# Gated linear attention with a seven-product matmul: sums of weights moved from GpSimd to VectorE, one weight load moved ahead of the operand fetches, small stores spread

## The chip, the cores and the metric

The kernel runs on one core of one Trainium2 chip. The core has TensorE (matmuls, results in PSUM banks), VectorE (DVE in the profile), ScalarE (ACT), GpSimd (POOL) and SyncE (SP), which here issues all DMAs, in one queue. The metric is the device time of one execution in microseconds.

## The reference

x is 2048 x 1024 float32. It is normalized by rows, and two branches read the result:

```python
xn = _layernorm(x, axis=-1)
s = _A_ref(xn, A_wqkv, A_w_phi, A_wo)      # attention branch
g = _silu(_B_ref(xn, B_w1, B_w3, B_w2))    # gated feed-forward branch
return x + s * g
...
# _A_ref: 32 heads of 32; phi_k likewise from k
pq = jnp.einsum("bhsd,hdf->bhsf", q, w_phi)
phi_q = jnp.concatenate([_softmax(pq, axis=-1), _softmax(-pq, axis=-1)], axis=-1)
kv = jnp.einsum("bhsf,bhsd->bhfd", phi_k, v)
z  = jnp.einsum("bhsf->bhf", phi_k)
o = num / den                              # phi_q with kv, and with z
...
# _B_ref: w1, w3 are 1024 x 3584, w2 is 3584 x 1024
h = _silu(gate) * up
out = jnp.einsum("bsf,fd->bsd", h, w2)
```

## The kernel before

Each float32 operand is split in two fp32r parts, hi and lo (`split`, L89 to L92: ScalarE copies hi, VectorE subtracts it from the source for lo), and a product is made in three passes: hi by hi, hi by lo, lo by hi. The large products use a scheme of seven products for a 2 x 2 block product instead of eight (`ORDER`): the left operands are A11, A12, S2, S1, S3, S4, A22, the right ones B11, B21, T2, T1, T3, B22, T4, where S and T are sums and differences of blocks. `b_sums` makes T3 and T2 out of raw blocks, and two more subtractions in `b_operands`, in place, make T1 and T4. All four stood on GpSimd.

Gate and up together are one 2 x 2 product. The 2048 rows come in two halves (tb), and in each half 28 blocks of 128 hidden columns (f) are worked through, seven products each, twelve matmuls of 128 x 512 a product. The 392 products are numbered as steps 0 to 391. At the start of the second half the products of its first two blocks alternate (`PAIRED`): steps 196, 197, 199 belong to block 0, step 198 is the first product (A11 with B11) of block 1, step 204 its fourth (S1 with T1). Partial results stay in PSUM banks a, b, c: bank b takes four of the seven products in turn, so between two of them a copy (h0, u0) on ScalarE or a sum on VectorE (u1, L631 before, L640 after) has to read it, else the next product waits.

From step 7 on every engine works in the order in which the program is written, step by step (`in_order`, `manual_schedule`): in a step first come the loads, then the matmuls, then splits of right operands four steps ahead (two ahead for block 1 of the second half), then side work, then the copies out of PSUM. The sums of a block stand two steps ahead of its first split (one step for blocks 1 and 2 of the second half). Raw weights (w1, w3) are loaded by `b_load` into the two buffers of pool rw, a block in advance.

Side work is laid between: normalizing and splitting the second half's x (`side_x`), folding the feature map into key and query weights (`side_fold`), sums and splits of key and value weights (`side_kv`) in the first half; the down weights (`side_w2`, 14 units of 11 steps; the first starts at step 197, raw blocks in tiles named room) and the output weights (`side_split`) in the second. `room(step, cost)` puts a piece on the first step whose VectorE work, by a table `base` and what was laid there already, leaves enough under a limit. At the turn between the halves `fetch` loads the second half's seven left operands, 2 MB each, into tiles that the first half's operands leave one by one.

Then come keys and values with 16 small matrices kv (`heads`, `kv_out`), the down product, with its own scheduler-given order, in rows r of eight pairs by seven groups (`product`; `a_first` loads h a row ahead), the queries and the output.

Of the kernel before, what the change touches and what calls it, by code (L numbers as in the profile page):

```python
# [17 lines left out]
P = 128  # L18
# [10 lines left out]
def tile_kernel(ctx: ExitStack, tc: tile.TileContext, x, wkT, wqT, wv, wphi, wo, w1, w3, w2, out):  # L29
# [94 lines left out]
    def b_sums(b11, b12, b22, t2):  # L124

        nc.gpsimd.tensor_sub(b12, b22, b12)
        nc.gpsimd.tensor_add(t2, b12, b11)
# [132 lines left out]
    def b_operands(rw, bo):  # L260
        b11, b21, b12, b22 = rw
        t2 = work.tile([P, 512], F, name="t2", tag="w")
        b_sums(b11, b12, b22, t2)
# [32 lines left out]
    b_gen = b_operands(rws.pop(0), bo)  # L296
# [8 lines left out]
    def first_folds(n):  # L305
        nonlocal at_fold
        for _ in range(n):
            wT, k, c, d = folds[at_fold]
            wr = early_w.pop(0) if early_w else load_w(wT, k, c, work.tile([P, 4, P], F, name="wr", tag="w"))
# [78 lines left out]
    HALF = 7 * NF  # L388
# [8 lines left out]
    for tb in range(2):  # L397
        for f in range(NF):
            own = [at_event[tb, f, j] for j in range(7)]
            steps = [k - LEAD for k in own]  # L400
            if (tb, f) == (1, 1):
                steps = [k - 2 for k in own]
            elif (tb, f) == (1, 2):
                steps = [own[0] + k for k in (-2, -2, -1, 0, 1, 2, 2)]
            if (tb, f) != (0, 0):
                for k in steps:
                    prep_at.setdefault(k, []).append((tb, f))
                sums_at.setdefault(steps[0] - (1 if tb and f in (1, 2) else 2), []).append((tb, f))
            late = divmod(NF * tb + f + 2, NF)
            if late[0] < 2:  # L410
                load_at.setdefault(max(steps[6] + 1, 0) if (tb, f) != (0, 0) else 0, []).append(late)

    base = {k: 0.7 * len(v) for k, v in prep_at.items()}
    for k, (tb, f, j) in enumerate(events):
        base[k + 1] = base.get(k + 1, 0) + (0, 0.7, 0, 0, 0.7, 1.4, 1.4 if f % 2 else 0.7)[j]
# [9 lines left out]
    def store_quad(step, d, src, name):  # L425

        step = room(step, 0.7)

        def f():
            t = qp.tile(list(src().shape[:1]) + [2] + list(src().shape[1:]), R, name=name, tag="q")  # L430
            split(t[:, 0], t[:, 1], src())
            at(step + 2, lambda: nc.sync.dma_start(d, t.bitcast(F)))
# [3 lines left out]
    def side_x(i, s0):  # L436
# [9 lines left out]
        for j in range(2):  # L446
            at_ = room(at_ + 1, 1.6)
# [14 lines left out]
        at_ = max(at_ + 1, s1 + 7)  # L462
        for m in range(3):
            at(at_ + m, lambda m=m: a_sums(a, nc.gpsimd, m))
        at_ += 1
# [3 lines left out]
    def side_kv(c, k, s0):  # L469
# [7 lines left out]
        at(s0 + 4, sums)  # L477
        at_ = s0 + 5
        for n in BNAMES:
            src = {"B11": 0, "B21": 1, "T2": 4, "T1": 0, "T3": 2, "B22": 3, "T4": 1}[n]  # L480
            at_ = store_quad(at_ + 1, wkv_d[c][n][:, :, k], lambda src=src: (r + t2)[src], "wkvo")
            if n == "B11":
                at(at_, lambda: nc.gpsimd.tensor_sub(r[0], r[3], t2[0]))
            elif n == "B21":
                at(at_, lambda: nc.gpsimd.tensor_sub(r[1], r[1], t2[0]))
# [22 lines left out]
    def side_w2(kb, kk, s0):  # L508
# [14 lines left out]
        at(s0 + 3, sums)  # L523
        at_ = s0 + 4
        for n in BNAMES:
            src = {"B11": 0, "B21": 1, "T2": 4, "T1": 0, "T3": 2, "B22": 3, "T4": 1}[n]
            at_ = store_quad(at_ + 1, w2_d[kb][n][:, kk], lambda src=src: r[src], "w2o")
            if n == "B11":
                at(at_, lambda: nc.gpsimd.tensor_sub(r[0], r[3], r[4]))
            elif n == "B21":  # L530
                at(at_, lambda: nc.gpsimd.tensor_sub(r[1], r[1], r[4]))
# [39 lines left out]
    for step, (tb, f, j) in enumerate(events):  # L571
# [108 lines left out]
    pkv = None  # L680

    def heads(i, xo, wb, steps, pend):
# [3 lines left out]
        for b, an, bn in ORDER:  # L686
# [19 lines left out]
            elif an == "S1":  # L706
                if pend:
                    kv(*pend)
                    if first:
                        kv_out(0, pkv)  # L710
# [13 lines left out]
            next(steps)  # L724
        return pkv, False, last, e1, v1

    def kv_out(c, pkv):
        kva = work.tile([P, 8, DH], F, name="kva", tag="w")
# [5 lines left out]
        for s in range(2):  # L734
            for j in range(4):
                sl = slice(32 * j, 32 * j + 32)
                nc.sync.dma_start(kv_d[j % 2, s, :, G * c + j // 2:G * c + G:2], kva[sl, 4 * s:4 * s + 4])
                nc.sync.dma_start(z_d[0, c, :, j, s].rearrange("g f -> f g"), zs[sl, 4 * s:4 * s + 4])

# [194 lines left out]
    for r, new in enumerate(steps):  # L934
# [156 lines left out]
```

## Time and profile before

| | us |
|---|---|
| median of 3 runs | 2465.31 (2465.04 to 2466.66) |
| the profiled execution, device time | 2466.53 |
| its span in the profile | 2464.8 |
| TensorE busy | 2406.8 (98%) |
| VectorE busy | 1748.6 (71%) |
| ScalarE busy | 887.4 (36%) |
| GpSimd busy | 681.8 (28%) |
| DMA | 521 MB moved, 211 GB/s mean |

The granted clock of TensorE was 0.996 of full speed in the mean. A line of a profile names the source line, the engine, the operation and the tiles as written<-read. In the view of groups the last column is the idle time of the engine before these instructions and who ended it; in the timeline the columns are start, duration, engine, line, operation, tiles, shape, count, and in brackets the idle time before and its releaser. A busy TensorE is not one at its peak, since matmuls are pipelined.

### The profile page before, as it was taken

To read this page: it belongs to the slowest core of one execution; us is meant where nothing else is said; L and a number is where in the kernel's file an instruction comes from. 1 tells how busy PE (TensorE), PEld (TensorE's weight loads), DVE (VectorE), ACT (ScalarE), POOL (GpSimd) and SP (SyncE) were. 2 spreads that over 40 slices of the span, in tenths; PEclk is the share of its full clock that TensorE was granted. 3 is DMA by queue.
4 is the path that set the end of the run, shared out by engine and by line. 5 is a ranking of instruction groups with operands and counts; after the bars stand their busy time and mean duration, and the time that the engine had idled before them with its cause. 6 is when DMAs were issued, how large, how long until landed. Compare 5 with 4: busy or idle time off the path is not lost.

```text
span 2464.8 us, 35933 instructions
## 1 busy us (share of the span) xinstructions
PE 2406.8 (98%) x13648; PEld 1971.2 (80%) x13648; DVE 1748.6 (71%) x2573; ACT 887.4 (36%) x1555; POOL 681.8 (28%) x481
## 2 busy tenths in 40 slices
PE   5999999999999999999999999999999999999999
PEld 5788788888788888888788788788888887777877
DVE  8578876664688888764566565687878887777775
ACT  6455544443354454432111113422222244222221
POOL 2334554432455555431000000011111112232222
PEclk9999999999999999999999999999999999999999
DMA  8556999775988887755967763623444376223222
GB/s 296 170 198 228 328 320 303 260 230 175 303 296 293 288 296 278 247 179 199 354 211 297 271 204 123 235 95 138 179 171 180 109 280 232 93 73 92 76 86 69
DMA packets 300812, 521.02 MB, mean 211 GB/s; under 512 B 24544, under 2 KB 172000, under 8 KB 298848
## 3 DMA queue, kind: packets, MB, share of 16 engines
q1 hardware_dynamic: 300640, 518.74, 61.1%
q8 instruction: 107, 1.75, 0.3%
q14 instruction: 65, 0.53, 0.1%
HBM read 331.22 MB, written 187.44 MB: 210 GB/s over the span
## 4 chain that ended last, share of the span: by engine, by line
PE 84%; DVE 6%; DMA 4%; SPq 2%; issue 2%; ACT 1%; POOL 1%; ACTq 0%; DVEq 0%; POOLq 0%
PE bankb L598 19%; PE pm L100 14%; PE bankb L915 12%; PE bankc L598 9%; PE bankb L692 7%; PE bankc L915 6%; PE banka L598 5%; PE bankc L692 3%; PE banka L915 3%; PE banka L692 2%; DVE bo L92 1%; PE po L1019 1%; PE pt L1013 1%; PE pkv L677 1%; DMA xoA<-xo_d0A 1%
## 5 line engine op out<-in xcount | busy, mean ns | idle before, releaser
L92 DVE TENSOR_TENSOR bo<-rw,bo 128x512 fp32r<-128x512 f32 x336 | 289.0, 863 | 214.9 <-ACT bo L91 212.6
L91 ACT CAST bo<-rw 128x512 fp32r<-128x512 f32 x336 | 206.9, 618 | 47.7 <-DMA rw<-in_w 8.8
L915 PE MATMUL bankb<-bo,as 128*128 128x512 f32 x816 | 201.6, 390 | 3.8 <-DVE acc L927 3.8
L925 POOL TENSOR_TENSOR acc<-acc,u 128x512 f32<-128x512 f32 x48 | 63.3, 1319 | 481.0 <-ACT u L924 472.6
L100 PE MATMUL pm<-wq,xh 128*128 128x512 f32 x768 | 185.7, 394 | 0.0
L270 POOL TENSOR_TENSOR rw<-rw,t 128x512 f32<-128x512 f32 x56 | 82.2, 1467 | 370.0 <-DVE bo L92 369.8
L915 PEld LDWEIGHTS bankb<-bo,as 128*128 128x128 f32 x816 | 153.3, 188 | 36.0 <-DVE acc L927 4.2
L598 PE MATMUL bankb<-op1A,bo 128*128 128x512 f32 x672 | 159.7, 393 | 8.9 <-ACT bo L91 4.7
L598 PE MATMUL bankb<-op0A,bo 128*128 128x512 f32 x672 | 160.9, 392 | 7.6 <-ACT bo L91 4.5
L598 PE MATMUL bankb<-op0S,bo 128*128 128x512 f32 x672 | 162.8, 391 | 4.8 <-ACT u L623 4.0
L100 PEld LDWEIGHTS pm<-wq,xh 128*128 128x128 f32 x768 | 141.9, 188 | 31.5 <-issue 3.0
L598 PE MATMUL bankc<-op0S,bo 128*128 128x512 f32 x672 | 163.0, 391 | 0.4 <-DVE op0S L92 0.3
L598 PE MATMUL bankb<-op1S,bo 128*128 128x512 f32 x672 | 161.6, 390 | 0.5 <-ACT u L623 0.5
L598 PE MATMUL bankc<-op1S,bo 128*128 128x512 f32 x672 | 161.2, 389 | 0.0
L598 PEld LDWEIGHTS bankb<-op1A,bo 128*128 128x128 f32 x672 | 126.7, 189 | 37.9 <-DVE u L631 6.0
L598 PEld LDWEIGHTS bankb<-op0A,bo 128*128 128x128 f32 x672 | 125.4, 188 | 34.6 <-ACT bo L91 4.7
L598 PEld LDWEIGHTS bankb<-op0S,bo 128*128 128x128 f32 x672 | 125.4, 188 | 31.7 <-ACT u L623 4.9
L598 PEld LDWEIGHTS bankb<-op1S,bo 128*128 128x128 f32 x672 | 126.0, 188 | 27.4 <-ACT u L623 1.2
L915 PE MATMUL bankc<-bo,as 128*128 128x512 f32 x576 | 147.3, 391 | 0.3 <-DVE as L92 0.3
L598 PEld LDWEIGHTS bankc<-op1S,bo 128*128 128x128 f32 x672 | 126.2, 188 | 26.2
L598 PEld LDWEIGHTS bankc<-op0S,bo 128*128 128x128 f32 x672 | 125.4, 188 | 26.7 <-DVE op0S L92 0.7
L884 POOL TENSOR_TENSOR ez<-e,zb 128x1024 f32<-128x1024 f32 x32 | 76.7, 2395 | 218.0 <-issue 122.9
(210 smaller groups left out, 4792.9 us busy)
## 6 DMA issues: line engine op xcount, KB each, us to landing
rw<-in_w SPq DMA_DIRECT2D x112, 512.0 KB, 4.6
hr<-h_d SPq DMA_DIRECT2D x56, 512.0 KB, 3.7
h_d<-h SPq DMA_DIRECT2D x111, 256.0 KB, 4.0
xoS<-xo_d0S SPq DMA_DIRECT2D x32, 512.0 KB, 8.7
xoS<-xo_d1S SPq DMA_DIRECT2D x32, 512.0 KB, 3.6
room<-in_w SPq DMA_DIRECT2D x56, 256.0 KB, 7.0
xoA<-xo_d0A SPq DMA_DIRECT2D x24, 512.0 KB, 9.6
xoA<-xo_d1A SPq DMA_DIRECT2D x24, 512.0 KB, 3.6
```

What stands on the lines that cost most here:

```text
L91: nc.scalar.copy(hi, src)
L92: (by or nc.vector).tensor_sub(lo, src, hi.bitcast(F))
L100: nc.tensor.matmul(p, xT[dch][:, a], w(dch, b), start=n == 0, stop=n == 3 * ND - 1)
L270: nc.gpsimd.tensor_sub(b11, b22, t2)
L598: nc.tensor.matmul(bank[b], bos[tb, f][bn][:, w, k], ao[an][:, u, k], start=first and n == 0, stop=LAST[b] == an and n == 11, skip_group_c ...
L677: nc.tensor.matmul(pkv[sl, m], e[:, m // 4, (m % 4) * P + 32 * h:(m % 4) * P + 32 * h + 32], v[:, 4 * (m % 4) + h], start=first and m == 0 ...
L692: nc.tensor.matmul(bank[b], xo[an][:, u, k], wb[bn][:, w, k], start=an in ("A11", "A12", "S1") and n == 0, stop=LAST[b] == an and n == 11, ...
L884: nc.gpsimd.tensor_mul(ez, ef, zb[c])
L915: nc.tensor.matmul(bank[b], t[:, u, pos + k], bos[kb, bn, k][:, w], start=first and n == 0, stop=LAST[b] == an and n == 5, skip_group_chec ...
L925: nc.gpsimd.tensor_add(c, c, u)
L1013: nc.tensor.transpose(pt[:, g, :], e[:, (4 * q + g) * P:(4 * q + g + 1) * P], ident)
L1019: nc.tensor.matmul(po[32 * g:32 * g + 32, hh, q * P:(q + 1) * P], kvu[sl, G * c + 4 * q + g], et[sl, g], start=True, stop=True, skip_group ...
```

## The change

The four sums of each block of gate and up are issued on VectorE, except for the blocks 0 and 1 of the first half, which stay on GpSimd; those of the down weights, of the key and value weights and of the second half's x go to VectorE everywhere. `base` now counts operations at 0.61 us each, two where a split is followed by a sum and two for a block's first sums; the limit in `room` goes from 2.4 to 2.55 us, and side sums ask for room, so side pieces stand on other steps than before. The last split of block 27 of the first half is made a step earlier, and with it the load of the raw weights of block 1 of the second half. The last nine folds at the start take their tiles from pool xp instead of work. `kv_out` returns four pieces of four stores, which are issued one at a time, and its tile kva takes the tag h1. Line numbers after differ from those before: `b_sums` is L127 and L128 (L126 and L127 before).

```diff
-    def b_sums(b11, b12, b22, t2):
-        nc.gpsimd.tensor_sub(b12, b22, b12)
-        nc.gpsimd.tensor_add(t2, b12, b11)
+    def b_sums(b11, b12, b22, t2, eng=None):
+        eng = eng or nc.vector
+        eng.tensor_sub(b12, b22, b12)
+        eng.tensor_add(t2, b12, b11)
...
             if n == "B11":
-                nc.gpsimd.tensor_sub(b11, b22, t2)
+                eng.tensor_sub(b11, b22, t2)
             elif n == "B21":
-                nc.gpsimd.tensor_sub(b21, b21, t2)
+                eng.tensor_sub(b21, b21, t2)
...
-    b_gen = b_operands(rws.pop(0), bo)
+    b_gen = b_operands(rws.pop(0), bo, nc.gpsimd)
...
-        first_folds(3)
+        first_folds(3, None)
...
-            if (tb, f) == (1, 1):
+            if (tb, f) == (0, NF - 1):
+                steps[6] -= 1
+            elif (tb, f) == (1, 1):
                 steps = [k - 2 for k in own]
...
-    base = {k: 0.7 * len(v) for k, v in prep_at.items()}
+    base, seen = {}, {}
+    for k in sorted(prep_at):
+        for g in prep_at[k]:
+            base[k] = base.get(k, 0) + (2 * OP_US if seen.get(g, 0) < 2 else OP_US)
+            seen[g] = seen.get(g, 0) + 1
+    for k, v in sums_at.items():
+        base[k] = base.get(k, 0) + 2 * OP_US * len(v)
...
-        while base.get(step, 0) + took.get(step, 0) + cost > 2.4:
+        while base.get(step, 0) + took.get(step, 0) + cost > 2.55:
...
     def side_w2(kb, kk, s0):
...
-        at(s0 + 3, sums)
-        at_ = s0 + 4
+        at_ = room(s0 + 4, 2 * OP_US)
+        at(at_, sums)
...
-            gens[g] = b_operands(rws.pop(0), bos[g])
+            gens[g] = b_operands(rws.pop(0), bos[g], nc.gpsimd if g == (0, 1) else None)
...
+            if out_now and not first:
+                out_now.pop()()
...
     def kv_out(c, pkv):
-        kva = work.tile([P, 8, DH], F, name="kva", tag="w")
+        kva = work.tile([P, 8, DH], F, name="kva", tag="h1", bufs=2)
...
+        def store(j):
+            sl = slice(32 * j, 32 * j + 32)
+            for s in range(2):
                 nc.sync.dma_start(kv_d[j % 2, s, :, G * c + j // 2:G * c + G:2], kva[sl, 4 * s:4 * s + 4])
                 nc.sync.dma_start(z_d[0, c, :, j, s].rearrange("g f -> f g"), zs[sl, 4 * s:4 * s + 4])
+        return [lambda j=j: store(j) for j in range(4)]
...
+        if out_now and r:
+            out_now.pop()()
         if r == 1:
             kv(*pend)
-            kv_out(1, pkv)
+            out_now += kv_out(1, pkv)
```

Three places in the order of instructions show it. The first is SP's queue at the turn; op1S and op1A are the fetched left operands, rw the raw weights of gate and up, room those of down, h_d a store of the first half. Before:

```order
L162 DMA op1S_5265<-xo_d1S_97 128x8x128 x4
L162 DMA op1S_5291<-xo_d1S_98 128x8x128 x4
L558 DMA h_d_6_64<-h_5130 128x4x128
L162 DMA op1S_5314<-xo_d1S_99 128x8x128 x4
L256 DMA rw<-in_w 128x1024
L257 DMA rw<-in_w 128x1024
L162 DMA op1S_5341<-xo_d1S_100 128x8x128 x4
L162 DMA op1A_5363<-xo_d1A_101 128x8x128 x4
L516 DMA room<-in_w 128x512 x4
```

and after:

```order
L163 DMA op1S_5265<-xo_d1S_97 128x8x128 x4
L163 DMA op1S_5294<-xo_d1S_98 128x8x128 x4
L257 DMA rw<-in_w 128x1024
L258 DMA rw<-in_w 128x1024
L567 DMA h_d_6_64<-h_5130 128x4x128
L163 DMA op1S_5317<-xo_d1S_99 128x8x128 x4
L163 DMA op1S_5341<-xo_d1S_100 128x8x128 x4
L163 DMA op1A_5363<-xo_d1A_101 128x8x128 x4
L527 DMA room<-in_w 128x512 x4
```

The raw weights of block 1 moved past one fetch and one store; the load of room keeps its place behind all fetches.

The second is VectorE's queue just after, between the h sum of step 200 (first row) and the u sum of step 203 (last row); bo is a right operand's lo part, w2o that of the down weights. Before:

```order
L620 TENSOR_TENSOR room<-banka,room 128x512
L92 TENSOR_TENSOR bo<-rw,bo 128x512 x2
L92 TENSOR_TENSOR w2o<-room,w2o 128x512
L92 TENSOR_TENSOR bo<-rw,bo 128x512
L92 TENSOR_TENSOR w2o<-room,w2o 128x512
L631 TENSOR_TENSOR u_5521<-bankb,u_5521 128x512
```

and after:

```order
L629 TENSOR_TENSOR room<-banka,room 128x512
L92 TENSOR_TENSOR bo<-rw,bo 128x512
L127 TENSOR_TENSOR room<-room 128x512
L128 TENSOR_TENSOR room<-room 128x512
L92 TENSOR_TENSOR bo<-rw,bo 128x512
L92 TENSOR_TENSOR w2o<-room,w2o 128x512
L538 TENSOR_TENSOR room<-room 128x512
L92 TENSOR_TENSOR bo<-rw,bo 128x512
L92 TENSOR_TENSOR w2o<-room,w2o 128x512
L539 TENSOR_TENSOR room<-room 128x512
L640 TENSOR_TENSOR u_5521<-bankb,u_5521 128x512
```

The four sums of the first unit of down weights came in; the second bo in this list is the split that step 204 reads.

The third is SP's queue in the first rows of the down product: kv_d and z_d are the small stores, hr is h, bo and late are down weights. Before, seven more pairs of small stores stand directly above these rows:

```order
L737 DMA kv_d<-kva 32x4x32
L738 DMA z_d<-zs 32x4x1
L769 DMA hr<-h_d_0_65 128x1024
L762 DMA bo<-w_d1T_189 128x1024 x2
L762 DMA late<-w_d1T_190 128x1024 x2
L769 DMA hr<-h_d_0_65 128x1024
```

and after, where the first row stands directly ahead of the stores:

```order
L776 DMA bo<-w_d1B_188 128x1024 x2
L749 DMA kv_d<-kva 32x4x32
L750 DMA z_d<-zs 32x4x1
L749 DMA kv_d<-kva 32x4x32
L750 DMA z_d<-zs 32x4x1
L783 DMA hr<-h_d_0_65 128x1024
L749 DMA kv_d<-kva 32x4x32
L750 DMA z_d<-zs 32x4x1
L749 DMA kv_d<-kva 32x4x32
L750 DMA z_d<-zs 32x4x1
L776 DMA bo<-w_d1T_189 128x1024 x2
L783 DMA hr<-h_d_0_65 128x1024
```

Two pairs of stores instead of eight are ahead of the load of h, and two more ahead of the next one.

More of the change, by code (lines that the diff above doesn't have):

```diff
@@ L303, in tile_kernel, with first_folds @@
     at_fold = 0
-    def first_folds(n):
+    def first_folds(n, t=lambda: work.tile([P, 4, P], F, name="wr", tag="w")):
         nonlocal at_fold
@@ L308, in first_folds @@
             wT, k, c, d = folds[at_fold]
-            wr = early_w.pop(0) if early_w else load_w(wT, k, c, work.tile([P, 4, P], F, name="wr", tag="w"))
+            wr = early_w.pop(0) if early_w else load_w(wT, k, c, t and t())
             pw = fold(wr, c)
@@ L423, in room, with store_quad @@
         return step
-    def store_quad(step, d, src, name):
-        step = room(step, 0.7)
+    def store_quad(step, d, src, name, then=None):
+        step = room(step, 2 * OP_US if then else OP_US)
         def f():
@@ L431, in f @@
             split(t[:, 0], t[:, 1], src())
+            if then:
+                then()
             at(step + 2, lambda: nc.sync.dma_start(d, t.bitcast(F)))
@@ L446, in side_x @@
         for j in range(2):
-            at_ = room(at_ + 1, 1.6)
+            at_ = room(at_ + 1, 1.3)
             at(at_, lambda j=j: stats(mv[0], j, xt[j]))
@@ L522, in side_w2 @@
         at(s0, load)
-        at(s0 + 3, sums)
-        at_ = s0 + 4
+        at_ = room(s0 + 4, 2 * OP_US)
+        at(at_, sums)
         for n in BNAMES:
             src = {"B11": 0, "B21": 1, "T2": 4, "T1": 0, "T3": 2, "B22": 3, "T4": 1}[n]
[L527 to L531, printed above, removed]
+            then = {"B11": lambda: nc.vector.tensor_sub(r[0], r[3], r[4]),
+                    "B21": lambda: nc.vector.tensor_sub(r[1], r[1], r[4])}.get(n)
+            at_ = store_quad(at_ + 1, w2_d[kb][n][:, kk], lambda src=src: r[src], "w2o", then)
     def side_store(m, s0):
@@ L709, in heads @@
                     if first:
-                        kv_out(0, pkv)
+                        out_now.extend(kv_out(0, pkv))
                 e1, v1 = room_ev()
```

30 lines of the change are left out of this document (12 added, 18 removed).

## The prediction

> **What bounds the kernel now.** I read four views: the busy time by stage, the chain of waits, the waits of TensorE in each stage, and the timeline around the long waits. The stages are start (0 to 85 us), first half of gate and up (85 to 625), turn (625 to 690), second half (690 to 1130), heads, first rows of the down product (1520 to 1560), rest. Columns: stage, its length, busy time and instructions by engine, granted clock, DMA share, GB/s.
> ```profile
> 0.00:85.00 85.00, 56.65 (x321) 48.07 (x322) 62.34 (x119) 48.90 (x90) 21.55 (x21) 0.94 0.85 286
> 85.00:625.00 540.00, 534.77 (x2425) 443.07 (x2424) 381.12 (x494) 245.71 (x443) 227.04 (x154) 1.00 0.75 246
> 625.00:690.00 65.00, 59.03 (x251) 47.47 (x250) 46.18 (x48) 26.29 (x49) 32.72 (x21) 0.97 0.90 290
> 690.00:1130.00 440.00, 436.61 (x1923) 360.14 (x1922) 335.00 (x397) 208.70 (x384) 214.93 (x142) 1.00 0.76 265
> ...
> 1520.00:1560.00 40.00, 35.86 (x211) 28.48 (x210) 19.59 (x40) 16.69 (x32) 0.00 (x0) 0.96 0.46 135
> ```
> TensorE is the bound. It idles 28.4 us at the start, 5.2 and 3.4 us in the halves, 6.0 at the turn and 4.1 in the last row (length less busy time). The change takes no matmul away, so those gaps, and the half clock behind the long ones, are all that it can win. The chain and the waits say what ends them:
> ```profile
> 102.31 5.44 PE bankb L598 x24
> ...
> PE bankb L598 <- ACT u L623: 3.0, 1, 3.0
> PE bankb L598 <- DVE u L631: 2.2, 3, 1.2
> ...
> PE bankb L598 <- ACT bo L91: 4.7, 1, 4.7
> PE bankb L598 <- DVE u L631: 0.7, 1, 0.7
> PE bankb L598 <- ACT u L623: 0.5, 1, 0.5
> ...
> PE bankb L598 <- DVE u L631: 3.4, 3, 1.6
> ```
> The first row gives the beat: 24 matmuls in 5.44 us, 2.72 us a product. Then come waits (total, times, longest) of the first half, the turn and the second half. All but the 4.7 are for a copy or sum that frees a bank. Ahead of the longest of the last row stands this:
> ```profile
> 990.02 0.68 DVE L92 TENSOR_TENSOR w2o<-room,w2o 128x512 fp32r<-128x512 f32 x1
> 990.62 1.77 DVE L92 TENSOR_TENSOR bo<-rw,bo 128x512 fp32r<-128x512 f32 x1
> ...
> 994.62 0.68 DVE L631 TENSOR_TENSOR u<-bankb,u 128x512 f32<-128x512 f32 x1
> ...
> 995.35 0.96 PE L598 MATMUL bankb<-op1A,bo 128*128 128x512 f32 x3 [1.57 <-DVE u L631]
> ```
> The same subtraction takes 0.68 us alone and 1.77 beside a GpSimd sum. Such stretched ones push the bank sum L631 late.
>
> **The sums on VectorE.** 320 sums of 128x512 leave GpSimd: four for each of 54 blocks of gate and up, 56 for the down weights, 32 for the value and key weights, 16 for x. What one costs there, and what its neighbours pay:
> ```profile
> L126 POOL TENSOR_TENSOR rw<-rw 128x512 f32<-128x512 f32 x56 | 93.7, 1674 | 55.6 <-DMA rw<-in_w 55.3
> ...
> L92 DVE TENSOR_TENSOR bo<-rw,bo 128x512 fp32r<-128x512 f32 x316 | 274.3, 871 | 204.1 <-ACT bo L91 201.9 <-DMA h_d<-h 1.2 <-DMA rw<-in_w 0.6
> L92 DVE TENSOR_TENSOR w2o<-room,w2o 128x512 fp32r<-128x512 f32 x98 | 90.5, 924 | 1.6 <-ACT w2o L91 1.3
> ...
> 54.30 2.50 DVE L92 TENSOR_TENSOR op0S<-xf,op0S 128x512 fp32r<-128x512 f32 x4
> ```
> No row shows such a sum on VectorE in these halves; the nearest is the subtraction of the same shape, 0.68 us, and four in a row start 0.60 us apart (2.50 less 0.69, by three). So a sum costs 0.60 to 0.69 us of VectorE; I take 0.61, as most neighbours are independent. 320 of them are 195 us. Against that the stretch goes: (871 - 680) x 316 ns = 60 us and (924 - 680) x 98 = 24 us in these two groups alone. VectorE stays near 385 of 540 us and 335 of 440.
>
> In the order the fullest blocks have 27 VectorE operations: 27 x 0.61 = 16.5 us of the 7 x 2.72 = 19.0 that a block takes. Counted step by step at 0.61 (waits for ScalarE's casts left out), no bank sum outside the turn comes late; the tightest has 0.17 us left. So the bank waits go: -5.2 in the first half, -1.2 at the turn (0.7 and 0.5), -3.4 in the second. At worst none of the 9.8 goes.
>
> **The turn.** Here are the gap, the weights' load (L256, L257), the first load of the down weights (L516), and their users:
> ```profile
> 606.00:651.00 45.00, 40.22 (x170) 32.51 (x169) 16.81 (x23) 14.66 (x27) 8.05 (x6) 0.96 1.00 301
> ...
> 611.56 6.72 SPq L162 DMA_DIRECT2D op1S<-xo_d1S  x4
> ...
> 626.21 1.34 SPq L256 DMA_DIRECT2D rw<-in_w  x1
> 627.60 0.44 SPq L257 DMA_DIRECT2D rw<-in_w  x1
> ...
> 632.87 0.62 ACT L91 CAST bo<-rw 128x512 fp32r<-128x512 f32 x1 [8.81 <-DMA rw<-in_w]
> 633.54 4.86 PE L598 MATMUL bankb<-op1A,bo 128*128 128x512 f32 x12 [4.68 <-ACT bo L91]
> 634.10 1.27 POOL L126 TENSOR_TENSOR rw<-rw 128x512 f32<-128x512 f32 x1 [15.61 <-DMA rw<-in_w]
> ...
> 642.29 2.86 SPq L516 DMA_DIRECT2D room<-in_w  x4
> 651.23 1.40 POOL L126 TENSOR_TENSOR room<-room 128x512 f32<-128x512 f32 x1 [10.88 <-DMA room<-in_w]
> 651.86 5.60 PE L598 MATMUL bankc<-op1S,bo 128*128 128x512 f32 x24
> ```
> SP is free at 611.56 + 6.72 = 618.3. Issued there, the weights land as long after issue as now (6.7 and 6.5 us): at 625.0 and 626.2. But the block's two sums now stand in VectorE's queue ahead of its first split, with two products of the old block between: 626.2 + five operations, 0.7 each, = 629.7. The product is due at 633.54 - 4.68 = 628.9, so TensorE waits 0.8 instead of 4.7, and the half clock behind it (4.86 us for twelve matmuls; 2.0 over the 2.88 of other products) goes.
>
> Then the step that the gain runs into. In the new VectorE order the first sums of the down weights (L127, L128) stand behind the split of step 201 and ahead of the split of T1 of block 1, which TensorE reads in step 204. Their data comes behind the same fetches, on the same queue, and the DMA engines are 1.00 busy from 606 to 651: the same bytes lie ahead, so it lands at 651.2 again, while GpSimd, which waited 10.9 us there and kept nobody, is out of it. Two sums and the split end at 651.2 + 0.7 + 0.7 + 0.7 = 653.3. TensorE, 0.8 late at 198, gets to 204 at 628.9 + 0.8 + 6 x 2.72 = 646.0 and waits 7.3 us; its half clock costs the same 2.0. Before, step 204 began at 651.86; now at 653.3, and runs 2.0 longer: +3.4 at this place. Ends of the unknown: no wait, if the load lands before 644, and 12 us, since VectorE is there at 637.9 + 1.4 = 639.3.
>
> The Trainium skill (TensorE: Matmul & The Clock Gate, Part 1, What's actually happening) says that an idle window of about 3.4 us halves the clock until a busy one has passed; by it 1.7 us would be lost instead of 2.0, and the sum would be 0.3 lower.
>
> **The small stores.** Eight pairs of stores stand on SP ahead of the load of h for the fifth row:
> ```profile
> 1523.04 0.32 SPq L737 DMA_DIRECT2D kv_d<-kva  x1
> ...
> 1534.42 0.38 SPq L769 DMA_DIRECT2D hr<-h_d  x1
> ...
> 1543.18 0.42 DVE L774 TENSOR_TENSOR sm<-hr 128x256 f32<-128x256 f32 x1 [10.02 <-DMA hr<-h_d]
> 1543.52 0.68 DVE L927 TENSOR_TENSOR acc<-bankb,acc 128x512 f32<-128x512 f32 x1
> ...
> 1544.26 2.23 PE L915 MATMUL bankb<-bo,as 128*128 128x512 f32 x6 [3.81 <-DVE acc L927]
> ```
> Now two pairs stand there (0.45 us each store): issued near 1525.0, and landing 8.7 us later as before, h is there at 1533.7, when VectorE asks for it (1543.18 - 10.02 = 1533.2). The 3.8 us go, and the half clock behind, 2.0: -5.8. Less than that, down to -3, if a later pair holds up the next load. The stores of the first half of the heads wait on nobody here: 0.
>
> **The start.** The last nine folds take their tiles from the other pool, so the second block's sums need not wait 11 us for a fold's store. But GpSimd's sum is slow there, and ScalarE's cast of that sum now stands ahead of the last casts of S1:
> ```profile
> 56.71 6.06 POOL L126 TENSOR_TENSOR rw<-rw 128x512 f32<-128x512 f32 x1 [26.45 <-DMA rw<-in_w]
> ...
> 60.97 1.31 ACT L91 CAST op0S<-xf 128x512 fp32r<-128x512 f32 x2
> ...
> 73.91 1.29 POOL L127 TENSOR_TENSOR t<-rw 128x512 f32<-128x512 f32 x1 [11.14 <-DMA wq_d<-wr]
> ```
> 56.71 + 6.06 + 1.3 = 64.1: S1's casts slip from 60.97 to about 65, which can cost TensorE 4 to 5 us, and the waits behind 61 us that it can win are about as many. I take 0, with -4 and +5 as ends.
>
> **The sum.** -5.2 - 1.2 - 3.4 + 3.4 - 5.8 + 0 = -12.2. The profiled execution took 2466.5 us (span 2464.8 and 1.7 around it), 1.2 above the median of 2465.3: 2454.3 there, 2453 as a median.
>
> **Rivals.** (a) The turn works: the down weights land before TensorE needs step 204. Then the turn wins 4.7 - 0.8 + 2.0 = 5.9 instead of losing 3.4: 2444. Against it stands the DMA share of 1.00 and the fixed place in the queue. (b) The bank waits stay, because VectorE gains as much work as it loses stretch: 9.8 us come back, 2463. The Trainium skill (Perfetto Trace Analysis, Optimizing Scalar/DVE Operations) says that moving work between VectorE and GpSimd might not help as they share a read port; the 0.68 against 1.77 above agrees on the port, but the sums leave it to one engine. (c) The start loses its 5 us: 2458. (d) Slower: VectorE takes its work strictly in order, so each of the 22 side sums that comes before its data holds bank sums back, as L774 held L927 above. At 1.0 us of TensorE for each, 22 us are lost: 2475; it decides from 12.2 / 22 = 0.55 us on. For it speaks the 43.2 us that GpSimd waited for these loads:
> ```profile
> L126 POOL TENSOR_TENSOR room<-room 128x512 f32<-128x512 f32 x14 | 20.2, 1442 | 43.2 <-DMA room<-in_w 43.2
> ...
> room<-in_w SPq DMA_DIRECT2D x56, 256.0 KB, 7.0
> ```
> Against it: but for the first, the sums stand four steps (10.9 us) or more behind the place of their loads, which land 7.0 us after issue in the median. The Trainium skill (TensorE: Matmul & The Clock Gate, the section on the 16 sub-arrays) says the same of the order: VectorE and ScalarE are strict FIFO.
>
> **Chances.** Forecast 0.45 (its own range 2448 to 2458), (a) 0.18, (b) 0.12, (c) 0.14, (d) 0.11. 0.2%, 4.9 us, is about what can be told from no change. Forecast, (a) and (c) lie below 2460.4: faster 0.77; (b) is no change, 0.12; (d) slower, 0.11. The range goes from (a) with 2 us beyond, 2442, to (b), 2463, and leaves out (d) and the far ends of the start.
>
> **What would show it.** Right: subtractions on VectorE near 0.69 us throughout both halves; no wait for a u sum above 1 us there; at the turn one wait of TensorE of about 7 us, on a split, with VectorE idle some 12 us before L127 on the load of the down weights, and step 198 nearly on time; no wait over 1 us in the first rows of the down product. Wrong: L127 without a wait there (then a), several waits at side sums (d), or waits for u sums as before (b).

## The result, and the profile after

| | before | changed |
|---|---|---|
| median of 14 runs each, us | 2466.04 (2465.04 to 2470.59) | 2466.32 (2464.23 to 2470.27) |
| profiled execution, us (span) | 2466.53 (2464.8) | 2464.45 (2462.7) |

The ratio is 1.0001, 95% interval 0.9993 to 1.0009: no change. 2453 was predicted, with a range of 2442 to 2463. The profiled executions differ by 2.1 us, more than the medians do; the changed kernel's was among the quicker of its runs.

The changed kernel by the same stages and columns as the view quoted of before:

```profile
0.00:85.00 85.00, 55.39 (x309) 48.27 (x310) 62.81 (x119) 47.74 (x88) 16.19 (x19) 0.90 0.83 285
85.00:625.00 540.00, 538.54 (x2447) 446.99 (x2446) 402.31 (x649) 248.43 (x448) 0.00 (x0) 1.00 0.74 248
625.00:690.00 65.00, 59.29 (x248) 48.17 (x247) 45.19 (x72) 26.05 (x49) 0.00 (x0) 0.95 0.89 292
690.00:1130.00 440.00, 439.88 (x1939) 363.69 (x1939) 345.36 (x537) 208.23 (x385) 0.00 (x0) 1.00 0.74 264
...
1520.00:1560.00 40.00, 33.82 (x138) 26.85 (x138) 17.39 (x33) 13.82 (x27) 0.00 (x0) 0.91 0.90 131
```

In the two halves the gaps of TensorE are gone: 1.5 us of 540 are left (5.2 before) and 0.1 of 440 (3.4 before). At the turn nothing is won (5.7 idle, 6.0 before). In the last row, the first rows of the down product, TensorE idles 6.2 us where it idled 4.1, and its clock is 0.91.

The waits of TensorE that stand behind that, from the view of waits of the changed kernel, in the order start, first half, turn, first rows of down (the second half has none):

```profile
PE bankc L607 <- ACT op0S L91: 4.1, 1, 4.1
...
PE pw L248 <- DMA wr<-in_wqT: 1.5, 1, 1.5
...
PE bankc L607 <- DVE bo L92: 5.4, 1, 5.4
PE bankb L607 <- DVE bo L92: 0.4, 1, 0.4
...
PE bankb L929 <- ACT acc L935: 5.2, 1, 5.2
PE bankb L929 <- DVE acc L941: 0.5, 1, 0.5
```

A second reading tells where the time went: the moment at which TensorE begins the same product in both programs, read from the timelines (for the last one, its last matmul). Changed less before, in us, from one profile each:

| place (time in the kernel before) | lead of before | gained here | forecast for it |
|---|---|---|---|
| third block, A12 (107.59) | +2.65 | start +2.65 | 0 |
| last block of the first half (625.98) | -2.20 | first half -4.85 | -5.2 |
| past the turn (710.74) | -1.64 | turn +0.56 | -1.2 + 3.4 |
| end of gate and up (1153.31) | -5.55 | second half -3.91 | -3.4 |
| first down product (1507.97) | -5.05 | heads +0.50 | 0 |
| last down product (2059.69) | -2.09 | small stores +2.96 | -5.8 |

8.8 us of the 10.1 between forecast (-12.2) and profile (-2.1) lie in the last row. The other rows vary too: in the five experiments below that keep the changed kernel's turn it cost 0.5 to 3.4 us, and in the five that keep its start that cost 0.8 to 2.9. For the last row, here are the stores, the loads of h, and who waits, from the timeline of the changed kernel:

```profile
1518.37 0.38 SPq L750 DMA_DIRECT2D z_d<-zs  x1
...
1519.79 0.38 SPq L783 DMA_DIRECT2D hr<-h_d  x1
...
1533.52 0.62 ACT L91 CAST af<-hr 128x512 fp32r<-128x512 f32 x1 [11.89 <-DMA hr<-h_d]
1534.04 0.61 ACT L91 CAST as<-hr 128x512 fp32r<-128x512 f32 x1
1534.56 0.58 ACT L935 COPY acc<-bankb 128x512 f32<-128x512 f32 x1
...
1535.19 2.93 PE L929 MATMUL bankb<-bo,as 128*128 128x512 f32 x6 [5.22 <-ACT acc L935]
```

The load of h does stand behind two pairs of stores only, and is issued at 1519.8: the forecast's 1525.0 less the 5 us that the whole program is ahead. But it needs 13.7 us to land, not 8.7. ScalarE stands at the cast of h, with the copy that frees TensorE's bank two places behind. The transfers of 1517 to 1546 us (packets and GB/s; the queue's packets, MB and share of the 16 DMA engines' time; the loads of h, with the median time from issue to landing):

```profile
DMA packets 2511, 2.99 MB, mean 103 GB/s; under 512 B 1808, under 2 KB 1808, under 8 KB 2510
...
q1 hardware_dynamic: 2510, 2.98, 81.3%
...
hr<-h_d SPq DMA_DIRECT2D x3, 512.0 KB, 13.7
```

The DMA engines are busy 81% of the time and move 103 GB/s; in the second half above, 0.74 of their time moves 264. The load of h issued at 1528.80 took 15.5 us.

### The profile page after: what moved, and what is told of

Same layout as the page of the kernel before. It is cut to its first block, busy times and chain, and to the rows that moved or that the text cites. A ratio compares the mean times of both kernels' runs of the same rounds, so it can differ in the third digit from the quotient of the medians.

```text
span 2462.7 us, 35712 instructions
## 1 busy us (share of the span) xinstructions
PE 2408.5 (98%) x13648; PEld 1975.4 (80%) x13648; DVE 1778.6 (72%) x2893; ACT 885.4 (36%) x1555; POOL 198.4 (8%) x161
## 4 chain that ended last, share of the span: by engine, by line
PE 91%; DMA 3%; DVE 1%; ACT 1%; issue 0%; SPq 0%; ACTq 0%; DVEq 0%
PE bankb L607 24%; PE pm L100 14%; PE bankc L607 12%; PE bankb L929 12%; PE bankb L701 7%; PE bankc L929 6%; PE banka L607 6%; PE bankc L701 3%; PE banka L929 3%; PE banka L701 2%; PE po L1035 1%; DMA hr<-h_d 1%; PE pt L1029 1%; PE pkv L686 1%; DMA xoA<-xo_d0A 1%; DMA op2T<-wkv_d0T 1%
## 5 line engine op out<-in xcount | busy, mean ns | idle before, releaser
L92 DVE TENSOR_TENSOR bo<-rw,bo 128x512 fp32r<-128x512 f32 x336 | 230.9, 688 | 156.7 <-ACT bo L91 155.6
L100 PE MATMUL pm<-wos,oT 128*128 128x512 f32 x576 | 136.2, 389 | 0.0
L929 PEld LDWEIGHTS bankc<-bo,as 128*128 128x128 f32 x576 | 108.0, 188 | 23.3 <-ACT acc L935 0.9
L100 PEld LDWEIGHTS pm<-wos,oT 128*128 128x128 f32 x576 | 108.0, 188 | 22.7 <-issue 0.2
```

Source lines behind the costliest of these rows:

```text
L92: (by or nc.vector).tensor_sub(lo, src, hi.bitcast(F))
L100: nc.tensor.matmul(p, xT[dch][:, a], w(dch, b), start=n == 0, stop=n == 3 * ND - 1)
L929: nc.tensor.matmul(bank[b], t[:, u, pos + k], bos[kb, bn, k][:, w], start=first and n == 0, stop=LAST[b] == an and n == 5, skip_group_chec ...
```

## The experiments

Each table of leads below is read as above, in us against the kernel before, from one profiled execution each. Times and ratios are of runs in rounds with the kernel before; the runs of one group share these. Each group ran on a chip of its own.

### Group 1: one part at a time (before: 2467.97 us, 21 runs)

**The stores whole again.**

```diff
-        return [lambda j=j: store(j) for j in range(4)]
+        for j in range(4):
+            store(j)
+        return []
```

> The changed kernel with the small stores whole again: all sixteen of a half issued at one place, as before. Theory S (the spread stores are what gave the gain back: cut in pieces of four they stand between the loads of h, and each such load lands 13.7 us after its issue instead of 8.7): TensorE again waits about 3.8 us once for a sum of the down product and no longer 5.2 us for a copy; the marks of the trace put the stores at +3.0 us, so the time falls by about 3 against the changed kernel's 2466.3, to 2463. Rival L (late loads of h come from the earlier arrival of the whole program at this place, and not from the stores' order): the wait stays near 5 us and the time at 2466.

Measured 2472.75 us, ratio 1.0028 (1.0015 to 1.0040). Neither theory said so: nothing is won, and the wait is 8.6 us, not 3.8 or 5. Against the first 14 runs of the changed kernel (1.0001) whole stores look worse than spread ones, against its later ones (1.0027, group 2) the same; which is dearer these runs do not tell. The waits, first rows of down and then heads:

```profile
PE bankb L931 <- DVE acc L943: 8.6, 1, 8.6
PE bankc L701 <- ACT ev L722: 3.5, 1, 3.5
```

The second place is new: there the stores of the first half stand, which cost nobody anything in the kernel before. So the spreading is not what gave the gain back: whole or spread, the stores cost more here than in the kernel before.

**The small stores on GpSimd's queue.**

```diff
-                nc.sync.dma_start(kv_d[j % 2, s, ...
-                nc.sync.dma_start(z_d[0, c, :, j, s] ...
+                nc.gpsimd.dma_start(kv_d[j % 2, s, ...
+                nc.gpsimd.dma_start(z_d[0, c, :, j, s] ...
```

> The changed kernel with the small stores issued by GpSimd on a queue of its own, in the same pieces. Theory S in its narrow form (the loads of h wait in SP's queue behind the small stores, which one queue works off in order): h lands about 7 us after its issue, as the loads of h ahead of the stores do (6.7 and 7.3), no wait over 1 us in the first rows of the down product, and the time falls by 5.2 us of wait, 0.9 of small waits and about 2 of half clock, to about 2458. Rival E (the DMA engines themselves are held by the small packets, whatever the queue): h still lands about 13 us after its issue, TensorE waits 5 us as in the changed kernel, and the time stays at 2466.

Measured 2458.41, ratio 0.9962 (0.9947 to 0.9977). The time is that of theory S, its reason only half. From the timeline (SP, GpSimd, TensorE) and, in the second fence, from the DMA view, the loads of down weights issued from 1524 to 1528 us, with their time from issue to landing:

```profile
1513.32 0.32 SPq L783 DMA_DIRECT2D hr<-h_d  x1
...
1518.89 0.55 POOL L749 DMA_DIRECT2D kv_d<-kva  x1 [24.07 <-ACT kva L741]
...
1548.60 1.66 PE L929 MATMUL bankb<-bo,as 128*128 128x512 f32 x6 [3.06 <-DVE acc L941]
```

```profile
late<-w_d1T SPq DMA_DIRECT2D x2, 512.0 KB, 14.8
```

SP no longer waits for kva, so the load of h goes out before the stores, at 1513.3, and the 5.2 us wait is gone. But loads issued among the stores still take 14.8 us, on a queue that no small store is in, and a wait of 3.1 us comes later. So the queue alone does not protect the loads, as rival E said, and the DMA engines themselves seem to be held. On this queue the trace records the stores in other packets (of 32 and 1024 bytes, and 256 of 4), and no run has rows of z on it, so it is not shown that the 4-byte stores do it here too. The Trainium skill (DMA: Bandwidth & Descriptors, Queues, rings and completion order) says that each DMA engine serves the queues in turn; by that a queue of its own does not keep loads free of such stores, and this trace agrees.

**The first unit of the down weights later.**

```diff
-        at_ = room(s0 + 4, 2 * OP_US)
+        at_ = room(s0 + (8 if (kb, kk) == (0, 0) else 4), 2 * OP_US)
```

> The changed kernel with the sums of the first unit of the down weights asked for eight steps behind their loads instead of four, so that they stand in step 205 or later; the other units stay. Theory T (VectorE is held at L127 by the load of these weights, with the split that step 204 needs behind it): the 5.4 us wait of TensorE at 649 goes with the half clock behind it, and nothing takes its place: 6 to 7.4 us less, 2459 to 2460. Rival (DMA engines that are busy all the time give the next wait at once): a wait for the next block's raw weights or for the operands takes at least 4 of the 5.4 us, and the time stays within 2 us of 2466.

**The folds' tiles as before.**

```diff
-        first_folds(3, None)
+        first_folds(3)
```

> The changed kernel with the last nine folds of the start taking their tiles from pool work again. Theory F (the other pool lets GpSimd's first sums of the second block run at 57 to 62 us instead of 57 to 75, so ScalarE's cast of that sum and the Silu behind it stand ahead of the last casts of S1, and TensorE waits 4.1 us for them): that wait goes, and the third block begins 2.65 us earlier, as in the kernel before; the time falls by 2.65 to about 2463.7. Rival (the start is slower because of GpSimd's own sums or the order the scheduler gives to the rest): the third block begins where it does in the changed kernel, at 110.2 us, and the time stays.

Measured 2462.86 (0.9981, 0.9972 to 0.9991) for the first and 2466.61 (0.9997, 0.9987 to 1.0006) for the second. The leads:

| | third block | end of first half | past the turn | end of gate and up | first down product | last |
|---|---|---|---|---|---|---|
| changed | +2.6 | -2.2 | -1.6 | -5.6 | -5.0 | -2.1 |
| w2 later | +2.1 | -2.7 | -8.4 | -12.1 | -9.2 | +0.2 |
| folds back | -1.0 | -5.8 | -5.2 | -9.2 | -8.8 | +0.4 |

Where they act, both did what their theories said: the turn now gains 5.6 instead of losing 0.6 (a wait of 2.7 us is left there), and the start is 3.6 better. But in the profiled executions it is all taken back, 2.9 us of the first by the heads and the rest by the down product. By the medians the first keeps 5.1 us against the kernel before, the second 1.4; the first's profiled run is the second slowest of its ten. The waits in the first rows of down, w2 later and then folds back:

```profile
PE bankb L929 <- ACT acc L935: 7.1, 1, 7.1
PE bankb L929 <- DVE acc L941: 3.1, 1, 3.1
```

```profile
PE bankb L929 <- ACT acc L935: 7.4, 1, 7.4
PE bankb L929 <- DVE acc L941: 3.9, 1, 3.9
```

### Group 2: what in the small stores it is (before: 2465.44 us, 16 runs)

**zs in one store**, in the order in which it lies; the stores of kva stay. This kernel leaves out the order of the heads, so its denominators are mixed up.

```diff
-                nc.sync.dma_start(z_d[0, c, :, j, s].rearrange("g f -> f g"), zs[sl, 4 * s:4 * s + 4])
...
+        nc.sync.dma_start(z_d[0, c].rearrange("g j s f -> (g j s f)").rearrange("(p e) -> p e", e=8), zs)
```

> The changed kernel with the eight stores of zs of each half, 128 packets of 4 bytes each, replaced by one store of 128 packets of 32 bytes; it leaves out that the values are put in the order of the heads, so the denominators are mixed up. The stores of kva stay, 128 packets of 128 bytes each. Theory Z (the 4-byte stores are what holds the loads of h: in the changed kernel each landing of z_d is the late one, 4.1 to 4.4 us behind the store before it, and loads behind them take up to 8.2 us for one packet): h lands within 8 us of its issue, no wait over 1 us in the first rows of the down product, and the time falls by 7 to 9 against the changed kernel in the same rounds. Rival K (any store of 128 small packets costs the same): half the stores are left, h lands about 11 us after its issue, and the time falls by 2 to 4.

Measured 2455.54 (2455.09 to 2455.69), ratio 0.9960 (0.9945 to 0.9975): 17 less than the changed kernel in the same rounds (2472.84, below), and 12.6 less in the spans. TensorE has no wait in the first rows of down. The stage, and the transfers of the same 29 us as above:

```profile
1520.00:1560.00 40.00, 40.00 (x178) 33.12 (x177) 23.72 (x46) 19.00 (x36) 0.00 (x0) 1.00 0.45 149
```

```profile
DMA packets 2738, 5.40 MB, mean 186 GB/s; under 512 B 1456, under 2 KB 1456, under 8 KB 2736
...
q1 hardware_dynamic: 2736, 5.38, 55.6%
...
hr<-h_d SPq DMA_DIRECT2D x4, 512.0 KB, 3.9
```

1456 packets under 512 bytes are left, most of them the 128-byte ones of kva, yet h lands in 3.9 us, and the engines move nearly twice the data in two thirds of the busy time. Theory Z holds, rival K does not, though the gain is twice what Z said. The trace of the changed kernel points the same way: its first two small stores, issued 0.4 us apart, take this long to land:

```profile
kv_d<-kva SPq DMA_DIRECT2D x1, 16.0 KB, 1.4
z_d<-zs SPq DMA_DIRECT2D x1, 0.5 KB, 5.4
```

The small packets are not what fills the busy time. By the packet records of these 29 us in the changed kernel, a packet of 4 bytes takes 9 ns in the median, but a 4 KB packet of the loads up to 8.2 us, where 1.4 us is the longest with zs in one store. It is the loads that are held.

**The sums alone**: the kernel before with the sums on VectorE and their places; folds, raw weights and small stores as before.

```diff
-            if (tb, f) == (0, NF - 1):
-                steps[6] -= 1
-            elif (tb, f) == (1, 1):
+            if (tb, f) == (1, 1):
...
-        first_folds(3, None)
+        first_folds(3)
...
-        kva = work.tile([P, 8, DH], F, name="kva", tag="h1", bufs=2)
+        kva = work.tile([P, 8, DH], F, name="kva", tag="w")
...
-        return [lambda j=j: store(j) for j in range(4)]
+        for j in range(4):
+            store(j)
+        return []
```

> The kernel before with the sums on VectorE and their places alone: folds of the start, load of raw weights at the turn and small stores as before. Theory H (the sums end the waits of the banks, and nothing else in the change does): by the marks of the trace 4.9 us less in the first half, 3.9 in the second, the start as before; 8 to 9 us ahead of the kernel before at the end of gate and up. What is left at the end depends on the stores: rival G (a program that comes earlier to the small stores only waits there for longer): under 3 us less in the end; without it 2457 to 2459 where the kernel before takes 2466.

Measured 2470.05, ratio 1.0020 (1.0011 to 1.0030). At the end of gate and up it leads by 9.8 us, a little above what theory H said, and it ends 3.4 behind: rival G, and more than it said. The heads take 8.4 back and the down product 5.1; the waits in the two:

```profile
PE bankc L698 <- ACT ev L719: 3.9, 1, 3.9
```

```profile
PE bankb L928 <- DVE acc L940: 9.2, 1, 9.2
```

**Three edits together**: w2 later, folds back, small stores on GpSimd's queue.

```diff
-        at_ = room(s0 + 4, 2 * OP_US)
+        at_ = room(s0 + (8 if (kb, kk) == (0, 0) else 4), 2 * OP_US)
...
-        first_folds(3, None)
+        first_folds(3)
...
-                nc.sync.dma_start(kv_d[j % 2, s, ...
+                nc.gpsimd.dma_start(kv_d[j % 2, s, ...
```

> The changed kernel with three edits at once: the first unit of the down weights eight steps behind its loads, the folds of the start with their tiles as before, the small stores on GpSimd's queue. Theory A (the three losses add up): from 9.5 us under the kernel before with the stores alone, 3.6 less from the start and 6 less from the turn, in all 17 to 20 us under the kernel before, 2447 to 2450. Rival G (the place of the small stores takes back what comes earlier, as it took back all of the 9 us that the folds and the turn had won): no more than 10 to 12 us under the kernel before, 2455 to 2458.

Measured 2446.90 (2443.85 to 2448.04), ratio 0.9923 (0.9909 to 0.9938): the losses add up, theory A. 2.4 us of wait are left in the first rows of down:

```profile
PE bankb L929 <- DVE acc L941: 2.4, 1, 2.4
```

**The changed kernel again.**

> The changed kernel once more, unchanged, in the rounds of the three others. By its 14 runs against 14 of the kernel before: within 0.1% of that. In the trace: if the wait in the first rows of the down product is a matter of the order of the stores alone, it is 5.2 us again; if it depends on when the small stores land in that run, it differs by some us, as 3.8 and 8.6 us did between the kernel before and the changed kernel with the stores whole.

Measured 2472.84 (2468.29 to 2473.90), ratio 1.0027 (1.0015 to 1.0038), against 1.0001 in the first 14 runs. The wait of 5.2 us is 7.8 here:

```profile
PE bankb L929 <- ACT acc L935: 7.8, 1, 7.8
PE bankb L929 <- DVE acc L941: 1.5, 1, 1.5
```

The same program in the same order, and its down product lost 6.0 us against the kernel before instead of 2.9. So the price of these stores differs from run to run (or by the chip, which these runs do not tell apart); 2.1 us of gain in one profile are no contradiction to a ratio of 1.0001 or of 1.0027.

### Group 3: without the 4-byte stores (before: 2468.06 us, 13 runs)

**Rows of z**: TensorE transposes zs, and two stores write it in 128-byte packets. One edit on the kernel before; the same lines go into three other kernels.

```diff
         nc.vector.tensor_copy(zs[:, 4:], pkv[:, 4:, DH])
+        zp = ps.tile([P, 512], F, name="zp", tag="kv", bufs=1)
+        zt = small.tile([8, P], F, name="zt")
+        nc.tensor.transpose(zp[:8, :P], zs, ident)
+        nc.vector.tensor_copy(zt, zp[:8, :P])
+        for s in range(2):
+            nc.sync.dma_start(z_d[0, c, :, :, s], zt[4 * s:4 * s + 4].rearrange("g (j f) -> g j f", j=4))
...
-                nc.sync.dma_start(z_d[0, c, :, j, s].rearrange("g f -> f g"), zs[sl, 4 * s:4 * s + 4])
```

> The kernel before with one edit: zs is transposed by TensorE into rows of 128 and stored by two stores of 16 packets of 128 bytes, in place of eight stores of 128 packets of 4 bytes in each half. Theory Z (the 4-byte stores alone hold the loads of h): the wait of 3.8 us of TensorE in the first rows of the down product goes, and the half clock behind it, 2.0: 5.8 less than the kernel before in the same rounds, and the time scatters by under 1 us from run to run instead of 5 to 8. Rival K (the eight stores of kva, whole and ahead of the load of h, are enough to make it late): 2 us or more of the wait stay, and the gain is under 3 us.

Measured 2461.23, ratio 0.9974 (0.9964 to 0.9984), 6.8 under the kernel before; the spans differ by 5.8. The wait is gone, with the stores of kva still whole and ahead of the load of h (the stage, then the landings of 1512 to 1546 us, as far as the trace tells them):

```profile
1520.00:1560.00 40.00, 40.00 (x239) 32.82 (x238) 23.61 (x49) 18.93 (x37) 0.00 (x0) 1.00 0.42 148
```

```profile
hr<-h_d SPq DMA_DIRECT2D x3, 512.0 KB, 5.5
...
kv_d<-kva SPq DMA_DIRECT2D x8, 16.0 KB, 1.5
```

The scatter did not go: 2458.66 to 2463.86 in ten runs. That half of the expectation fell; what else makes runs differ stays open.

**The three edits with rows of z**: w2 later, folds back, rows of z; the stores of kva spread on SP's queue.

```diff
-        at_ = room(s0 + 4, 2 * OP_US)
+        at_ = room(s0 + (8 if (kb, kk) == (0, 0) else 4), 2 * OP_US)
...
-        first_folds(3, None)
+        first_folds(3)
...
+        nc.tensor.transpose(zp[:8, :P], zs, ident)
```

> The changed kernel with three edits: the folds of the start with their tiles as before, the first unit of the down weights eight steps behind its loads, and zs stored in rows as in the run on the kernel before; the stores of kva stay spread on SP's queue. If the losses add up: the three edits with GpSimd's queue gave 2446.9 with 2.4 us of wait left in the first rows of the down product; without that wait 2444 to 2445, 20 to 22 us under the kernel before. If the stores on GpSimd's queue were the better place, because SP's queue then does not wait for kva: 2447 or more.

Measured 2443.37 (2442.73 to 2444.86), ratio 0.9902 (0.9887 to 0.9917): 24.7 us under the kernel before, the best of all. Turn, second half and first rows of down:

```profile
625.00:690.00 65.00, 65.00 (x288) 53.80 (x287) 45.72 (x72) 29.82 (x55) 0.00 (x0) 1.00 0.79 255
690.00:1130.00 440.00, 440.00 (x1939) 363.33 (x1938) 348.08 (x542) 208.91 (x386) 0.13 (x1) 1.00 0.77 270
...
1520.00:1560.00 40.00, 40.00 (x178) 33.14 (x177) 23.06 (x45) 17.06 (x32) 0.00 (x0) 1.00 0.32 105
```

**The sums alone with rows of z**: the run of the sums alone, with the lines above.

```diff
+        nc.tensor.transpose(zp[:8, :P], zs, ident)
```

> The kernel before with the sums on VectorE and their places, and zs stored in rows; nothing else of the change. With the 4-byte stores the sums alone came 8 us earlier to the end of gate and up and ended 4 to 5 us later than the kernel before. Theory (the sums' gain is real, and the small stores took it): it now stays, 8 to 9 us under the run of the kernel before with rows of z alone, 13 to 15 under the kernel before. Rival (what VectorE gains in gate and up it loses later for another reason): within 2 us of the kernel before with rows of z alone.

Measured 2454.89, ratio 0.9948 (0.9933 to 0.9963): 6.3 under the kernel before with rows of z, 13.2 under the kernel before. The sums' gain is real, though 2 us less than expected: it is 8.0 at the end of gate and up, and 5.9 at the first down product; what takes the rest back in the heads stays open.

**All edits, stores of kva whole.**

```diff
-        kva = work.tile([P, 8, DH], F, name="kva", tag="h1", bufs=2)
+        kva = work.tile([P, 8, DH], F, name="kva", tag="w")
...
-        return [lambda j=j: store(j) for j in range(4)]
+        for j in range(4):
+            store(j)
+        return []
```

> The run with all three edits and rows of z, but with the stores of kva whole, all eight of a half at one place. Theory Z (order and number of the small stores do not matter once none is of 4 bytes): within 1.5 us of the run with the stores of kva spread. Rival K (whole stores ahead of the load of h make it late): 2 to 6 us slower than that run, with a wait of TensorE in the first rows of the down product.

Measured 2445.15 (2443.04 to 2447.38), ratio 0.9908 (0.9894 to 0.9923), against 0.9902 for the spread ones, with intervals that overlap; the medians differ by 1.8, a little over what theory Z allowed, the spans by 0.4, and the first rows of down have no wait. Spreading is worth nothing that these runs can tell.

One number holds the group together. From the first matmul of its first product to the last of its last, the down product takes, against the kernel before:

| | us |
|---|---|
| rows of z on before; all edits; sums alone; all with whole stores | -5.9, -6.0, -6.0, -6.0 |
| zs in one store | -6.1 |
| small stores on GpSimd's queue; three edits with these | -2.7, -1.8 |
| changed, twice; stores whole; sums alone | +2.9, +6.0, +4.3, +5.1 |
| w2 later; folds back | +9.4, +9.2 |

So the 4-byte stores cost the kernel before 6 us here, the changed kernel 9 to 12, and kernels that came some 9 us earlier 15. That it is the earlier arrival that makes them dearer is not shown: the same program, run twice, lies 3 us apart, and the one with the stores whole came only 0.3 us earlier and paid 10.

## Why the prediction was wrong

- **Small stores, -5.8.** This is the step that failed, and 8.8 us of a miss of 10.1. It said: issued near 1525.0, and landing 8.7 us later as before. Issued at 1519.8, it landed 13.7 us later. The 8.7 had been measured behind all sixteen stores, with SP held up among them by landings of earlier ones:

```profile
SPq L737 <- DMA kv_d<-kva: 3.2, 2, 2.7
```

  It was taken for the latency of a load at any place in that queue. With the 4-byte stores gone the same load lands in 5.5 us, so part of the 8.7 was already theirs, and a load issued earlier among them meets more of it. The forecast counted stores ahead of the load in the queue, at 0.45 us of issue each, and never asked how long the stores under way hold a load. In the rows of before it could be seen: all sixteen stores carry 132 KB together and take from 1523 to 1540 us to issue and land. The remark "down to -3, if a later pair holds up the next load" looked at the right thing, but put it at 2.8 us.
- **The stores of the first half, 0.** True of the changed kernel, but on a cover that the forecast did not name: with these stores whole and the sums on VectorE, 3.5 and 3.9 us of wait arise there. The trace names no releaser for the copy that was late; with rows of z the wait does not occur.
- **The sums, -5.2 and -3.4.** Right: -4.85 and -3.91, and no wait for a u sum left. The group of splits shows the reason as forecast, 688 ns instead of 871:

```profile
L92 DVE TENSOR_TENSOR bo<-rw,bo 128x512 fp32r<-128x512 f32 x336 | 230.9, 688 | 156.7 <-ACT bo L91 155.6 <-DMA h_d<-h 0.3
```

  VectorE's busy time rose by 21 us in the first half and 10 in the second (402.3 and 345.4), where the forecast had them near 385 and unchanged at 335. Its own rows, 195 us of sums against 84 of stretch, gave neither; the rest came back from groups that it did not count, such as the product h<-h,u, 996 ns before and 692 after. Rivals (b) and (d) did not happen: the one wait of the first half is for a fold's load.
- **The turn, +3.4 and -1.2.** Right in its mechanism, row by row. Step 198 came 0.4 late (0.8 forecast); then this:

```profile
647.13 0.69 DVE L127 TENSOR_TENSOR room<-room 128x512 f32<-128x512 f32 x1 [9.04 <-DMA room<-in_w]
...
648.47 0.69 DVE L92 TENSOR_TENSOR bo<-rw,bo 128x512 fp32r<-128x512 f32 x1
...
649.21 7.02 PE L607 MATMUL bankc<-op1S,bo 128*128 128x512 f32 x17 [5.36 <-DVE bo L92]
```

  TensorE waits 5.4 us at step 204 instead of 7.3: the down weights landed at 647.1, which is 4.1 earlier than forecast, and 2.2 of these are the lead that the whole program has here. The half clock behind it costs more than the 2.0 of the sum: it lasted 6.83 us, 6.17 of them with matmuls, which at half speed is some 3 us (an estimate from this row; the clock is the 0.50):

```profile
648.55:655.38 6.83, 6.17 (x15) 4.81 (x16) 5.60 (x10) 1.69 (x4) 0.00 (x0) 0.50 0.45 107
```

  The forecast's side remark that the sum could be 0.3 lower changes only this half clock; the stores' one, also taken at 2.0, would move the sum as much the other way. With these sums later, the turn wins 5.6 us.
- **The start, 0 of -4 to +5.** It cost 2.6, by the mechanism of rival (c), now shown: GpSimd's sums end at 62.2, ScalarE's cast of them and the table load and Silu behind it stand ahead of the last casts of S1:

```profile
62.19 0.62 ACT L91 CAST bo<-t 128x512 fp32r<-128x512 f32 x1 [2.13 <-POOL t L128]
...
63.38 1.28 ACT L630 ACT_TABLE_LOAD   x1
64.67 0.63 ACT L630 ACTIVATE h<-h 128x512 f32<-128x512 f32 x1
65.21 1.12 ACT L91 CAST op0S<-xf 128x512 fp32r<-128x512 f32 x2
```

  Undone, the third block begins 3.6 us earlier.
- **The chances.** "No change" came, at 0.12, but not by its rival: the bank waits went, and the stores took their gain. The forecast had no rival in which the stores' place became worse. That the total came out so near to zero is chance: the gains of the halves and the losses at the start and the stores happen to be of one size.

## What to carry to other kernels

A latency read behind a crowd of transfers belongs to that crowd: before you move a load among small stores, read what the DMA engines move in that stretch and how long they are busy for it, not only the queue's order. Gain won upstream is only kept if the next place that waits on a transfer lets it through, so follow the lead over the old kernel from stage to stage to the end; here one edit downstream decided whether 8 to 10 us of gain in gate and up made the kernel 0.2% slower or 0.5% faster (1% with the rest mended). A transposing matmul and two row stores were cheaper here than 1024 writes of 4 bytes, by 6 us or more of the down product.

## What the runs showed of the hardware

With eight stores of 128 packets of 4 bytes, 4 KB in all, and as many stores of 128-byte packets between them, two 512 KB loads issued among them landed only after 13.7 and 15.5 us. With rows of z or zs in one store the loads of h in these rows take 3.2 to 7.0, with 1024 packets of 128 bytes still there. From another queue the small stores still go with loads of 14.8 us. No run has the 4-byte stores without the others. The Trainium skill (DMA: Bandwidth & Descriptors, Specifications) gives 512 bytes as the least transfer for full rate, below which a DMA engine reads, modifies and writes. 128 and 4 bytes are both below it, and only the 4-byte ones were seen to cost TensorE anything; here the measurement decides. How such a store holds the loads' packets no run shows.
